# Another set of rank offsets for the scheduler of a Fourier filter with a gated convolution

## The chip, the cores and the metric

The kernel runs on one core of a Trainium2 chip. The metric is the device time of one execution, in microseconds (us). A profile is one further execution recorded by the hardware profiler; its span runs from the first to the last instruction.

## What is computed

x has 8 batches of 3200 positions and 256 channels. Each batch goes through a real Fourier transform along the positions, a complex 256x256 product with a bias, a soft threshold and the transform back; then through a gated product:

```python
X = np.fft.rfft(x, axis=1)
Yr = Xr @ w_r - Xi @ w_i + b_r
Yi = Xr @ w_i + Xi @ w_r + b_i
Y = soft(Yr, 0.01) + 1j * soft(Yi, 0.01)
y = np.fft.irfft(Y, n=3200, axis=1)
gate = sigmoid(sum over k < 5 of conv_w[k] * y shifted by 4 - k)
out = (gate * (y @ w_val)) @ w_out
```

`w_val`, `conv_w` and `w_out` arrive as float64 and are turned into float32 on the chip by integer steps.

## The kernel before, in words

The transform of 3200 points is split into 64 times 50. For each batch b there are three parts.

- **p1**, 8 pieces: x is loaded (`load`, L577), multiplied by `f1_sb` (L583), copied to SBUF by ScalarE (L588) and stored to `a_dram` (L597).
- **p2**, 13 units, u = 0 to 12, of two frequencies each (the last has one): `a` is loaded back once for two units (L615), multiplied by `f2_sb` (`s2`, L634), split into a high and a low half (L684 to L696), multiplied by the complex weights (`mix_sum` L709, `mix` L704; in the last unit L667 and L668), biased (L715, L718), thresholded (L722, L724), and for every second unit multiplied by `g1_sb` (`s1i`, L747; the last unit L739), copied (L758, L755) and stored to `z_dram` (L765).
- **p3**, 8 blocks k of four: z is loaded (L788), multiplied by `g2_sb` (`positions`, `s2i`, L803) and copied to `y_sb` (L810), of which there is one for all batches. `taps` forms the convolution for one or two blocks (first tap on ScalarE L857, four more for each half on VectorE L860, sigmoid L871). `gated` splits y into high and low (helper `split`, L360 and L362), forms val (`matrix`, L835, or whole in float32, L831), multiplies it by the gate on VectorE (L902), splits that product and multiplies it by `w_out` (project, L835 or L831), copies it (L926, the last block L920) and stores it (L928, L924).

The program order on every engine is not written out by hand. `Plan` collects pieces (engine, modelled duration, what they need, which tile they open) and lays them in an order by a greedy list simulation: for each engine it takes, of the pieces that could start within a slack (20 ns on the computing engines, 50 ns on SP) of the earliest, the one with the smallest rank `at`. The engine whose piece starts first goes next. The rank is the unit's place, b * 13 + u, plus an offset from the dictionary `O`. The simulation also holds the slots of each tile kind (`SLOTS`; two for `ps_2`, which p1, z, y_p, val and project tiles share), eight DMAs under way, a limit on DMA backlog for pieces with a rank above -27, the price of going between quadrant and full-array matmuls (`SWITCH`), and a model of how the matrix engine's instructions are fetched: in packets of 256, asked for 130 instructions into a packet, at 5200 ns each plus a share of the DMA backlog.

Offsets have the name of the step: `p1` and `p1_step` for the first products, `load_x`, `load_a`, `load_z` for loads on SP, `s2`, `mix_sum`, `s1i` within p2, `p3` for the start of the third part, and relative to it `y` (split), `conv` (taps), `val`, `gate` (gate product and its split) and `project`. A name with a number belongs to that batch and is added. `later` ranks the float64 conversion, `turn` the making of `g1_sb`. `together` favours staying in quadrant mode, `stay` widens the slack in that mode, `hold` holds back a lone quadrant piece when fewer than `crowd` are near. `late_val` and `late_out` are indices into the list `LATE` of the blocks of batches 6 and 7, from which on val and project take the whole float32 weights; at 7 and 15 that is the last block of batch 6 and all of batch 7 for val, and the last block of batch 7 for project.

```python
lone = e == "PE" and sum(c[1]["mode"] == "q" for c in near) < O["crowd"]
if e == "PE" and mode == "q":
    stay = max(SLACK[e], 100 * min(O["stay"], 4.0))
...
start, p = min(near, key=lambda c: (c[1]["at"] + (0.0 if e != "PE" or c[1]["mode"] != "q" else -O["together"] if mode == "q"
                                                   else O["hold"] if lone else 0.0), c[0]))
...
p1(b, u, (b - 1) * T + O["p1"] + O.get(f"p1_{b}", 0.0) + u * O["p1_step"])
...
start = (b + 1) * T + O["p3"] + O.get(f"p3_{b}", 0.0)
...
positions(b, k, start + (i - 1) * T / NB)
```

Of the kernel before, what the change touches and what calls it, by code (L numbers as in the profile page):

```python
# [83 lines left out]
class Plan:  # L84
# [11 lines left out]
    def add(self, at, engine, busy, fn, uses=(), sets=(), new=None, delay=None, mode="r", kb=0, chain=None, extra=0, moves=1, ways=16, ins=0):  # L96
        n = len(self.pieces)
        before = set()
        for key in uses:
            before |= set(self.writers.get(key, ()))  # L100
        for key in sets:
            before |= set(self.readers.get(key, ())) | set(self.writers.get(key, ()))
        for key in uses:
            self.readers.setdefault(key, []).append(n)
        for key in sets:
            self.writers[key], self.readers[key] = [n], []
        p = dict(n=n, at=round(at, 5), engine=engine, busy=busy, fn=fn, before=before, new=new or {}, mode=mode, kb=kb, extra=extra, moves=moves, ways=ways, ins=ins,
                 tiles={key[:2] for key in (*uses, *sets)}, delay=busy + LAND[engine] if delay is None else delay)
        p["behind"] = {self.last[chain]} if chain in self.last else set()
        if chain:  # L110
            self.last[chain] = n
        self.pieces.append(p)
        return n

    def order(self):
# [42 lines left out]
        while len(done) < len(pieces):  # L158
            best = None
            for e in engines:  # L160
# [13 lines left out]
# [4 lines that stand above are left out]
                    near = [c for c in could if c[0] <= first + (stay if c[1]["mode"] == "q" else SLACK[e])]  # L178
                start, p = min(near, key=lambda c: (c[1]["at"] + (0.0 if e != "PE" or c[1]["mode"] != "q" else -O["together"] if mode == "q"
                                                                   else O["hold"] if lone else 0.0), c[0]))  # L180
                if best is None or start < best[0]:
# [68 lines left out]
def act(n, kind="copy"):  # L250
# [3 lines left out]

NU = (NT + 1) // 2
T = float(NU)
O = {'stay': -42.085,
     'crowd': -50.453,
     'hold': 7.335,
     'together': 155.775,  # L260
     'later': 18.484,
     'load_x': 192.178,
     'p1': -1.787,
     'p1_step': 1.293,
     'load_a': -41.005,
     's2': -2.447,
     's1i': 2.145,
     'p3': 2.825,
     'load_z': -29.254,
     'y': 3.704,  # L270
     'conv': 5.188,
     'val': 5.514,
     'gate': -19.992,
     'project': 8.565,
     'late_val': 7.079,
     'late_out': 15.503,
     'turn': -153.706,
     'mix_sum': -0.971,
     'p1_1': -89.715,
     'load_x_1': 85.875,  # L280
     'p1_2': 25.498,
     'p3_6': -1.759,
     'p3_7': -0.606,
     'y_7': 18.885,
     'conv_7': -29.176,
     'val_7': 13.441,
     'gate_7': -17.01,
     'project_7': 13.598,
     'p3_1': -0.93,
     'p1_3': -6.723,  # L290
     'p3_0': 0.056}
WARM = 4, 1, 19
SLOTS = {"x": 3, "zl": 3, "y_hl": 2, "s1": 3, "a": 2, "xs": 2, "sx": 2, "xz": 1, "yb": 2, "tp": 3, "zst": 2,
         "acc": 2, "g_hl": 2, "o": 2, "ps_s2": 2, "ps_y": 1, "ps_k": 2, "ps_2": 2, "a_dram": 2, "z_dram": 2}
# [6 lines left out]
def fourier_filter_then_gated_conv(ctx: ExitStack, tc: tile.TileContext, x, w_r, w_i, b_r, b_i,  # L301
# [5 lines left out]
    dram = ctx.enter_context(tc.tile_pool(name="dram", bufs=2, space=bass.MemoryType.DRAM))  # L307
    LATE_VAL, LATE_OUT = set(LATE[int(O["late_val"]):]), set(LATE[int(O["late_out"]):])
    plan = Plan(SLOTS)
# [80 lines left out]
    def from_float64(at, n, views, uses, done, new=None, first=None):  # L390
# [34 lines left out]
        for k, (fn, busy) in enumerate(steps):  # L425
            def piece(k=k, fn=fn):
                if k == 0 and first:
                    first()
                fn()
            add(at + O["later"] + 0.12 * k, "DVE", busy, piece, uses, done, new if k == 0 else None, delay=busy + (130 if k == 12 else 0))  # L430

# [599 lines left out]
```

## Time and profile before

| | |
|---|---|
| three runs | 883.49, 883.22, 881.55 us (median 883.22) |
| profiled execution | 881.59 us, of which the span is 879.8 |
| mean granted clock of the matrix engine | 0.994 |
| busy: PE, DVE, ACT | 857.8, 759.1, 604.9 us |
| DMA | 163.34 MB, mean 186 GB/s |

PE is the matrix engine's matmuls, PEld its weight loads, which overlap them; DVE is VectorE, ACT ScalarE, POOL GpSimd, SP the engine whose queue issues most DMAs. L835 is line 835 of the kernel. A group of instructions is given as line, engine, operation, out<-in, shapes and count, then busy time and mean ns of one, then idle time of the engine before them and who ended it. A wait row reads: who waited, for whom, us in all, times, longest. A row of the timeline has start, length, engine, line and how often the operation follows itself. "issue" is time in which an engine waited for nothing that the profile shows. Ends of matmuls are modelled, so a busy PE may hide slack.

### The profile page before, as it was taken

The numbers are of one execution on the slowest core, as the hardware profiler recorded it, in microseconds if no ns is written. First come the engines' busy times: TensorE is split into PE (matmuls) and PEld (weight loads), VectorE is DVE, ScalarE is ACT, GpSimd is POOL, SyncE is SP. The second block draws the span as 40 slices with busy tenths as digits, with TensorE's granted clock in tenths as the row PEclk, the third lists the DMA queues.
The fourth block names the chain that finished last, engine by engine and source line by source line (L and its number), as shares of the span: only waits on it lengthen the run. The fifth ranks groups of instructions, "written<-read, shape, count | busy, mean of one in ns | idle before, by whom it ended". The sixth has DMA issues, their size and how long they took to land.

```text
span 879.8 us, 24544 instructions
## 1 busy us (share of the span) xinstructions
PE 857.8 (97%) x10400; PEld 745.5 (85%) x10400; DVE 759.1 (86%) x1143; ACT 604.9 (69%) x928; POOL 3.8 (0%) x11
## 2 busy tenths in 40 slices
PE   7999999999999999999999999999999999998997
PEld 3778788878999898898899889898899999998775
DVE  2346888999989996999879997899969999899796
ACT  2456666977677766877667776877658775875664
POOL 0000000000000000000000000000100000000000
PEclk9999999999999999999999999999999999999999
DMA  6878886786554476565855576646746353423522
GB/s 212 253 244 253 240 269 197 265 251 199 165 184 146 148 218 212 177 185 172 272 168 171 175 237 205 218 122 208 244 133 202 104 171 94 142 103 110 186 76 94
DMA packets 105289, 163.34 MB, mean 186 GB/s; under 512 B 9690, under 2 KB 78172, under 8 KB 105180
## 3 DMA queue, kind: packets, MB, share of 16 engines
q1 hardware_dynamic: 103764, 158.43, 58.1%
q10 hardware_dynamic: 1416, 3.34, 1.2%
q8 instruction: 82, 1.34, 0.6%
q14 instruction: 27, 0.22, 0.1%
HBM read 82.05 MB, written 79.69 MB: 184 GB/s over the span
## 4 chain that ended last, share of the span: by engine, by line
PE 78%; DVE 15%; DMA 3%; ACT 2%; issue 1%; SPq 0%; ACTq 0%; DVEq 0%
PE y_ps L704 14%; PE o_ps L835 12%; PE v_ps L835 11%; PE s L634 9%; PE z_ps L747 8%; PE k_bank L709 7%; PE y_p L803 6%; DVE acc L860 6%; PE p L583 5%; DMA x<-in_x 2%; PE warm L951 1%; DVE acc L902 1%; PE v_ps L831 1%; DMA f_sb<-in_f 1%; DVE gated L362 1%
## 5 line engine op out<-in xcount | busy, mean ns | idle before, releaser
L860 DVE SCALAR_TENSOR_TENSOR acc<-y_sb,cw_sb,acc 128x800 f32<-128x800 f32 (+1 forms) x264 | 258.7, 1017 | 11.4 <-ACT acc L857 11.2
L704 PE MATMUL y_ps<-w_sb,xs 128*128 128x256 f32 x1152 | 157.7, 286 | 0.7 <-DVE yb L718 0.7
L835 PE MATMUL o_ps<-gated,wo_sb 128*128 128x400 f32 x756 | 153.5, 352 | 0.0
L704 PEld LDWEIGHTS y_ps<-w_sb,xs 128*128 128x128 f32 x1152 | 144.3, 190 | 8.6 <-issue 3.9
L835 PEld LDWEIGHTS o_ps<-gated,wo_sb 128*128 128x128 f32 x756 | 135.6, 189 | 3.4 <-issue 1.0
L835 PE MATMUL v_ps<-y_hl,wv_sb 128*128 128x400 f32 x660 | 130.6, 346 | 1.1 <-ACT y_sb L810 1.1
L634 PEld LDWEIGHTS s<-f_sb,a 128*128 128x128 f32 x800 | 100.3, 191 | 24.9 <-issue 19.0
L835 PEld LDWEIGHTS v_ps<-y_hl,wv_sb 128*128 128x128 f32 x660 | 118.7, 188 | 2.1 <-ACT y_sb L810 1.3
L634 PE MATMUL s<-f_sb,a 128*128 128x128 f32 x800 | 111.9, 280 | 1.3 <-DVE xs L692 1.2
L747 PE MATMUL z_ps<-tp,g_sb 64*64 64x256 f32 x1536 | 93.7, 380 | 0.0
L688 ACT CAST xs<-s 128x512 fp32r<-128x512 f32 x96 | 56.2, 586 | 43.0 <-PE y_ps L704 28.1
L709 PE MATMUL k_bank<-w_sb,xs 128*128 128x256 f32 x576 | 85.3, 283 | 0.4 <-DVE yb L715 0.4
L722 ACT ACTIVATE tp<-yb,nlam 128x512 f32<-128x512 f32 (+1 forms) x104 | 73.6, 708 | 16.5 <-DVE yb L718 9.0
L718 DVE TENSOR_TENSOR yb<-y_ps,yb 128x512 f32<-128x512 f32 x96 | 65.4, 681 | 19.9 <-PE y_ps L704 19.7
L747 PEld LDWEIGHTS z_ps<-tp,g_sb 64*64 64x64 f32 x1536 | 57.1, 133 | 27.1 <-issue 5.8
L360 ACT CAST gated<-acc 128x800 fp32r<-128x800 f32 x63 | 54.2, 861 | 37.1 <-DVE acc L902 33.5
L709 PEld LDWEIGHTS k_bank<-w_sb,xs 128*128 128x128 f32 x576 | 74.8, 188 | 5.1 <-issue 1.1
L926 ACT COPY o<-o_ps 128x800 f32<-128x800 f32 x63 | 51.9, 823 | 38.0 <-PE o_ps L835 37.8
L803 PEld LDWEIGHTS y_p<-g_sb,zl 50*64 50x64 f32 x4096 | 66.1, 135 | 13.9 <-issue 5.1
L902 DVE TENSOR_TENSOR acc<-v_ps,acc 128x800 f32<-128x800 f32 x64 | 62.9, 983 | 16.9 <-PE v_ps L835 14.1
L724 DVE SCALAR_TENSOR_TENSOR tp<-yb,tp 128x512 f32<-128x512 f32 (+1 forms) x104 | 68.8, 661 | 7.7 <-ACT tp L722 7.4
L803 PE MATMUL y_p<-g_sb,zl 50*64 50x50 f32 x4096 | 71.8, 220 | 3.4 <-issue 2.2
(80 smaller groups left out, 1028.4 us busy)
## 6 DMA issues: line engine op xcount, KB each, us to landing
zl<-z_dram SPq DMA_DIRECT2D x128, 200.0 KB
out<-o SPq DMA_DIRECT2D x63, 400.0 KB
a_dram<-s SPq DMA_DIRECT2D x120, 208.0 KB
a<-a_dram SPq DMA_DIRECT2D x96, 256.0 KB
z_dram<-z_t SPq DMA_DIRECT2D x48, 512.0 KB
x<-in_x SPq DMA_DIRECT2D x120, 200.0 KB
a_dram<-s ACTq DMA_DIRECT2D x8, 208.0 KB
x<-in_x ACTq DMA_DIRECT2D x8, 200.0 KB
```

The lines of the kernel that those rows point to most:

```text
L634: nc.tensor.matmul(spec()[:, c, :, i, :], tl[ka][:, i0 + i, c * P:(c + 1) * P], f2_of(i), start=True, stop=True)
L688: nc.scalar.copy(out=tl[kx][:, 0:512], in_=tl[k2].rearrange("p a b -> p (a b)"))
L704: nc.tensor.matmul(p[:, 1 - r, :], xm(hx, c, r), w_sb[:, m, hw, c, :], start=k == 0, stop=k == 5)
L709: nc.tensor.matmul(p, sm(hx, c), w_sb[:, 0, hw, c, :], start=k == 0, stop=k == 5)
L718: add(at + 0.2, "DVE", dve(2 * D), lambda: nc.vector.tensor_tensor(out=yb(), in0=tl[ky], in1=yb(), op=ALU.add), [ky + (0,)], [kb + (0,)])
L722: nc.scalar.activation(out=buffer(kt, "tp", [P, 2, D])[:, 0:n], in_=tl[kb][:, 0:n], func=AF.Relu, bias=nlam)
L724: add(at + 0.2, "DVE", dve(n * D), lambda: nc.vector.scalar_tensor_tensor(out=tl[kt][:, 0:n], in0=tl[kb][:, 0:n], scalar=LAM, in1=tl[kt][: ...
L747: nc.tensor.matmul(p[e * HP:(e + 1) * HP, i, j * D:(j + 1) * D], g[i * HP:(i + 1) * HP, r, e * HP:(e + 1) * HP], tl[kts[j]][i * HP:(i + 1) ...
L803: nc.tensor.matmul(pv[h][e * HP:(e + 1) * HP, c, m, :], zt[half(h), m, c * P + e * HP:c * P + (e + 1) * HP], g2_sb[half(h), :], start=True ...
L835: nc.tensor.matmul(p[:, e, 0:TB], w[:, hw, c, e * P:(e + 1) * P], src(hy, c), start=n == 0, stop=n == 5)
L860: nc.vector.scalar_tensor_tensor(out=acc(c), in0=y_of(c, j), scalar=cw_sb[:, c, j:j + 1], in1=acc(c), op0=ALU.mult, op1=ALU.add)
L902: add(at + own("gate", b), "DVE", dve(2 * TB), lambda: nc.vector.tensor_tensor(out=gate(), in0=hn(tl[kv][:, :, 0:TB]), in1=gate(), op=ALU. ...
```

## The change

Only numbers in `O` change. The pieces, their instructions and sizes, the slots and the simulation stay as they are; the order in which the simulation lays them out is another. `late_val` and `late_out` keep their values, so the same blocks take the whole weights.

```diff
-O = {'stay': -42.085,
-     'crowd': -50.453,
-     'hold': 7.335,
-     'together': 155.775,
-     'later': 18.484,
-     'load_x': 192.178,
-     'p1': -1.787,
-     'p1_step': 1.293,
-     'load_a': -41.005,
-     's2': -2.447,
-     's1i': 2.145,
-     'p3': 2.825,
-     'load_z': -29.254,
-     'y': 3.704,
-     'conv': 5.188,
-     'val': 5.514,
-     'gate': -19.992,
-     'project': 8.565,
+O = {'stay': -60.503,
+     'crowd': -102.979,
+     'hold': 18.379,
+     'together': 205.778,
+     'later': 86.272,
+     'load_x': 124.016,
+     'p1': -1.441,
+     'p1_step': 1.544,
+     'load_a': -11.084,
+     's2': -1.909,
+     's1i': 2.258,
+     'p3': 0.441,
+     'load_z': -50.245,
+     'y': 8.904,
+     'conv': 9.838,
+     'val': 5.628,
+     'gate': -16.483,
+     'project': 7.913,
      'late_val': 7.079,
      'late_out': 15.503,
-     'turn': -153.706,
-     'mix_sum': -0.971,
-     'p1_1': -89.715,
-     'load_x_1': 85.875,
-     'p1_2': 25.498,
-     'p3_6': -1.759,
-     'p3_7': -0.606,
-     'y_7': 18.885,
-     'conv_7': -29.176,
-     'val_7': 13.441,
-     'gate_7': -17.01,
-     'project_7': 13.598,
-     'p3_1': -0.93,
-     'p1_3': -6.723,
-     'p3_0': 0.056}
+     'turn': -139.497,
+     'mix_sum': -0.639,
+     'p1_1': -49.829,
+     'load_x_1': 76.138,
+     'p1_2': 56.402,
+     'p3_6': 1.34,
+     'p3_7': 3.039,
+     'y_7': 106.034,
+     'conv_7': -43.292,
+     'val_7': 14.22,
+     'gate_7': -25.153,
+     'project_7': 14.981,
+     'p3_1': 0.545,
+     'p1_3': -48.761,
+     'p3_0': -0.433}
```

## The prediction

> **What bounds the kernel now.** I read the page first, then busy time by stretches, then who waited for whom on the matrix engine and on VectorE in the last 80 us, then the instructions around the waits found there. The page's head gives the span and the shares:
>
> ```profile
> span 879.8 us, 24544 instructions
> PE 857.8 (97%) x10400; PEld 745.5 (85%) x10400; DVE 759.1 (86%) x1143; ACT 604.9 (69%) x928; POOL 3.8 (0%) x11
> ```
>
> The stretches (length, then busy time of PE, weight loads, DVE, ACT, POOL; then clock, DMA share and GB/s) show three regimes:
>
> ```profile
> 0.00:80.00 80.00, 71.24 (x484) 49.63 (x484) 31.47 (x56) 34.50 (x64) 1.14 (x9) 0.96 0.81 238
> 80.00:120.00 40.00, 39.30 (x396) 31.59 (x393) 33.14 (x76) 26.82 (x47) 0.00 (x0) 1.00 0.83 259
> 120.00:160.00 40.00, 39.51 (x616) 33.50 (x615) 34.95 (x67) 27.38 (x48) 0.00 (x0) 1.00 0.74 221
> 160.00:240.00 80.00, 78.53 (x855) 67.59 (x850) 76.66 (x112) 59.88 (x91) 0.00 (x0) 1.00 0.71 218
> 240.00:720.00 480.00, 479.18 (x6195) 433.38 (x6195) 440.65 (x648) 355.43 (x542) 2.69 (x2) 1.00 0.60 184
> ...
> 720.00:760.00 40.00, 39.81 (x614) 37.20 (x616) 36.67 (x59) 25.24 (x40) 0.00 (x0) 1.00 0.44 139
> 760.00:800.00 40.00, 39.71 (x484) 36.72 (x480) 39.91 (x52) 30.63 (x43) 0.00 (x0) 1.00 0.29 100
> 800.00:824.00 24.00, 20.05 (x285) 17.50 (x278) 18.21 (x23) 12.81 (x17) 0.00 (x0) 0.93 0.48 159
> 824.00:872.00 48.00, 46.70 (x491) 36.12 (x489) 46.22 (x56) 30.87 (x41) 0.00 (x0) 1.00 0.30 106
> 872.00:880.00 8.00, 3.76 (x14) 2.22 (x13) 1.21 (x2) 1.32 (x2) 0.00 (x0) 0.93 0.27 102
> ```
>
> From 240 to 720 PE stands idle for 0.8 us of 480: PE bounds it. From 760 DVE is full (39.91 of 40), has a hole of 5.8 us between 800 and 824, and is nearly full again until 872 (46.22 of 48): the last batch's end is bound by DVE, with PE close beside it. The first 240 us hold 11.4 us of PE idle time, 8.8 of them in the first 80. A sequence can win only in those idle times and in what hides inside busy time. Who waited in the last 80 us, PE first, then DVE:
>
> ```profile
> PE z_ps L739 <- DVE acc L902: 2.9, 1, 2.9
> PE y_p L803 <- issue: 1.3, 2, 1.0
> ...
> DVE acc L860 <- ACT acc L857: 4.2, 2, 3.5
> DVE o L920 <- DMA out<-o: 3.7, 1, 3.7
> ```
>
> **What the change leaves alone.** The instructions are the same, so the sum of their durations is too. Of the 35 offsets many cannot act. `stay` is negative in both, so the slack stays at 20 ns; with `crowd` below zero `lone` is never true and `hold` is unread; `together` (156, now 206) exceeds the difference of priorities among work that is ready together. `y_7` is unread, since batch 7's val products all lie in the late list, which needs no split. The x loads are last on SP in both (124 and more against at most about 130 for the last output, which comes batches later), `turn` is first in both, `p1_1` stays ahead of, and `p1_2` behind, everything ready beside it. `later` pushes the float64 conversion behind still more work, but at 25.6 it already stood behind nearly all of batch 1's middle (13 to 26), and DVE idles 6.9 us between 80 and 120. Each of these I cost at nothing.
>
> **What it does change, as places in one batch of 13 units.** Adding `p3` to the offset, in units from the batch's start: positions 2.8 to 0.4, val 8.3 to 6.1, project 11.4 to 8.4 (all earlier on PE); the y split 6.5 to 9.3 and the taps 8.0 to 10.3 (later on ACT and DVE); the gate product -17.2 to -16.0. For batch 6 with its own offset: y 4.8 to 10.7, taps 6.3 to 11.6, val 6.6 to 7.4, positions 1.1 to 1.8, project hardly. Batch 7: positions 2.2 to 3.5, taps -21.8 to -30.0, val and project two later, still in the same order. First products (p1) are spread over 7 steps of 1.54 and not 1.29. On SP the z loads go from behind the next batch's a loads to ahead of them, and batch 0's a loads come under the backlog limit.
>
> A unit in time: the single last-z product closes the p2 part of batches 5 and 6 at these starts, 99.4 us apart, so 7.6 us a unit.
>
> ```profile
> 610.67 0.59 PE L739 MATMUL z_ps<-tp,g_sb 128*128 128x256 f32 x2
> 710.07 0.59 PE L739 MATMUL z_ps<-tp,g_sb 128*128 128x256 f32 x2
> ```
>
> **SP.** PE never waits for a landing behind the start: its waits for DMA are x at 1.7 and f at 1.2 us in all, both before 60 us, and batch 0's a loads, with a priority of -11 and up, still go ahead of the f2 parts beside them (0.1 and up). The cover for the later a loads is the queue of ready val and project work. If it is gone, one late load costs what the f transfer cost, 1.2. I take 0, with 0 to +1.2.
>
> ```profile
> PE p L549 <- DMA x<-in_x: 1.7, 2, 1.0
> ...
> PE k_bank L469 <- DMA f_sb<-in_f: 1.2, 1, 1.2
> ```
>
> **Mode runs in the middle.** PE alternates between full-array pieces and quadrant pieces (p1, z, y_p). What one excursion costs is read from neighbouring starts:
>
> ```profile
> 691.50 1.05 PE L634 MATMUL s<-f_sb,a 128*128 128x128 f32 x8
> 692.31 2.42 PE L835 MATMUL v_ps<-y_hl,wv_sb 128*128 128x400 f32 x12
> ...
> 696.68 1.05 PE L634 MATMUL s<-f_sb,a 128*128 128x128 f32 x8
> 697.66 1.15 PE L803 MATMUL y_p<-g_sb,zl 50*64 50x50 f32 x64
> ...
> 720.34 1.96 PE L747 MATMUL z_ps<-tp,g_sb 64*64 64x256 f32 x32
> 722.22 0.97 PE L709 MATMUL k_bank<-w_sb,xs 128*128 128x256 f32 x6
> ```
>
> ```profile
> 300.58 1.96 PE L747 MATMUL z_ps<-tp,g_sb 64*64 64x256 f32 x32
> 302.36 1.04 PE L583 MATMUL p<-x,f_sb 50*64 50x512 f32 x8
> ```
>
> The s piece lasts 0.81 us until a full-array piece starts and 0.98 until a quadrant piece does; z lasts 1.78 until p and 1.88 until a full-array piece. An excursion so costs 0.17 + 0.10 = 0.27 us. Between the two L739 rows above there are nine runs, from this first one (618.57) to the y_p at 697.66:
>
> ```profile
> 618.57 1.09 PE L583 MATMUL p<-x,f_sb 50*64 50x512 f32 x8
> ```
>
> That is 2.4 us a batch. Nine runs serve 22 quadrant pieces, and the two slots of `ps_2`, which every one of these pieces and every val and project tile needs, keep a run to two or three pieces. The new steps bring p1 and positions nearly in line: p1 at -1.4, 0.1, 1.6, 3.2 ..., positions at -1.2, 0.4, 2.1, 3.7 ..., so that pairs get likelier. I take one run fewer in each of four settled batches, -4 x 0.27 = -1.1 us; bounds one run more or two fewer in seven batches, +1.9 to -3.8.
>
> **Issue stalls.** Long trains of small matmuls run the queue dry: after 157 records of y_p this row waits 1.02 us for nothing but issue.
>
> ```profile
> 817.57 2.77 PE L803 MATMUL y_p<-g_sb,zl 50*64 50x50 f32 x157
> 821.35 0.78 PE L803 MATMUL y_p<-g_sb,zl 50*64 50x50 f32 x35 [1.02 <-issue]
> ```
>
> Over the span PE lost 2.2 us so:
>
> ```profile
> PE y_p L803 <- issue: 2.2, 5, 1.0
> ```
>
> An order rated over three packet times should break up the worst train; I take -0.4 (a third of the tail's 1.3), bounds -2.2 to +2.2, since as many new ones can arise. The Trainium skill's page "Runtime: NRT & Kernel Launch", section "Instruction fetch mechanics", has it that crossing a block of instructions is mostly hidden. By that rule this term would be 0 and the sum 0.4 us higher; the 1.02 us row speaks against it for dense trains.
>
> **The tail.** Batch 7's positions need all of z, and batch 6's taps must have read `y_sb`, which exists once. The wait of DVE is this one:
>
> ```profile
> 823.90 4.90 DVE L860 SCALAR_TENSOR_TENSOR acc<-y_sb,cw_sb,acc 128x800 f32<-128x800 f32 x5 [3.55 <-ACT acc L857]
> ```
>
> With batch 6's taps and splits 5.3 to 5.9 units (40 us and more) later in rank, batch 7's p2 instructions go ahead of them on DVE, the last z comes earlier, and some of batch 6's DVE work is left to fill the hole while z goes to memory and back. I take half the 3.55, -1.8 us; bounds: both waits gone, -3.55 - 2.9 = -6.5, and two further waits of the kind of L739's, +5.9. What is late next is the val tile's slot, and DVE itself, which has 1.8 us left between 824 and 872.
>
> Startup and fill (0 to 240): p1 of batch 3 goes from 17.5 to -24 and starts runs of its own. I take 0, between -2.6 (all the idle time from 80 to 240) and +1.4 (five more runs).
>
> **The sum**: -1.1 - 0.4 - 1.8 = -3.3 us. The profiled execution took 881.59 (span 879.8 and 1.8 around it) and would take 878.3; the median of the three runs is 883.22, 1.6 higher, so the forecast is 879.9.
>
> **Rivals.** *Slower: val tiles park in the two slots.* Val waits for its y split, the taps come after, and a val tile holds one `ps_2` slot until L902 has multiplied it, which needs taps and sigmoid. Before, taps (8.0) were ahead of val (8.3); after, val can run when the split is done (9.3) and the taps stand at 10.3: 0.9 units, 7 us, in which one of two slots may be held and PE waits for each evacuation. The trace has one such case, the 2.9 us of L739. It decides when DVE is full while the tile waits, as in 760 to 800. Two more in the tail, or one in each of two full batches, give 883.2 + 5.9 = 889; one gives 886. Against it: 240 to 720 has almost no such wait, and every other val finds its taps within what DVE can spare (39 of 480 us idle). Chance 0.28.
>
> *No change.* The hole is a round trip (last z, store, load, y_p, copy, first tap) that no rank shortens, and the middle is full: 883.2. That much of the list is unread, and the changed sequence is then nearly the old one, is the same case. Chance 0.22.
>
> *Much faster.* PE's busy 97% may hide slack: from 240 to 720 weights load for 433 of 480 us. If a better order reclaimed a tenth of the 46 us between, and the tail both waits, it is -4.6 - 6.5, 872; with half the tail, 875. The Trainium skill's page "Perfetto Trace Analysis", section "Identifying the Most-Contended Engine", judges PE by weight-load share, 85% here, and not by matmul share; that rule points this way. Against it, from the page's groups (busy, mean ns):
>
> ```profile
> L747 PE MATMUL z_ps<-tp,g_sb 64*64 64x256 f32 x1536 | 93.7, 380 | 0.0
> ...
> L747 PEld LDWEIGHTS z_ps<-tp,g_sb 64*64 64x64 f32 x1536 | 57.1, 133 | 27.1 <-issue 5.8
> ```
>
> z alone streams 36.6 us longer than its weights load, over the span, and any order keeps that. Chance 0.10.
>
> **How the numbers follow.** Forecast 0.40, much faster 0.10, no change 0.22, slower 0.28. A measurement of this kernel tells about 0.2%, 1.8 us. Faster 0.50, same 0.22, slower 0.28. The likeliest case alone is 877 to 881.5; for eight in ten the range runs from 874 (into the much faster case) to 888 (two slot waits short of their full price), which holds also the bounds of the runs term.
>
> **What would show it.** Right: between 800 and the end the wait of L860 for L857 at about half, the last L739 starting some us before 804, eight runs between two L739 rows, the y_p issue wait under 2. Wrong: PE idle time above 2 us between 240 and 720, or new waits for L902 (slots); the last L739 at 804 or later; a DVE idle time before 760 larger than now, with more taps behind it.

## The result, and the profile after

The changed kernel is slower: 885.48 us (median of 12, 880.81 to 892.98) beside 880.45 for the kernel before, a ratio of 1.0056 [1.003, 1.0082]. Its profiled execution took 887.27, of which the span is 885.3, at a mean granted clock of 0.986 where the kernel before had 0.994. The time lies in the forecast range of 874 to 888, and the direction is the opposite of the forecast. The head of the page after:

```profile
span 885.3 us, 24513 instructions
PE 860.8 (97%) x10400; PEld 747.2 (84%) x10400; DVE 759.8 (86%) x1143; ACT 602.8 (68%) x928; POOL 4.4 (1%) x11
```

The shares say nothing of the 5.5 us: PE is at 97% in both. The stretches do (length, then busy time of PE, weight loads, DVE, ACT, POOL; then clock, DMA share, GB/s). After:

```profile
120.00:160.00 40.00, 37.57 (x588) 29.88 (x591) 31.57 (x61) 26.15 (x44) 0.00 (x0) 1.00 0.65 200
160.00:200.00 40.00, 38.51 (x461) 31.29 (x454) 38.19 (x56) 31.09 (x47) 0.00 (x0) 0.96 0.76 236
...
240.00:720.00 480.00, 475.70 (x6192) 430.04 (x6191) 440.75 (x646) 353.64 (x536) 3.30 (x2) 1.00 0.60 183
...
760.00:800.00 40.00, 39.79 (x511) 37.10 (x511) 39.68 (x59) 28.78 (x45) 0.00 (x0) 1.00 0.29 98
800.00:840.00 40.00, 37.27 (x455) 32.04 (x455) 33.53 (x39) 25.58 (x32) 0.00 (x0) 0.91 0.46 151
840.00:880.00 40.00, 38.79 (x341) 30.16 (x340) 36.24 (x45) 22.75 (x31) 0.00 (x0) 1.00 0.20 73
```

Between 120 and 160 PE was idle for 0.5 us before and for 2.4 now. In the settled stretch, 240 to 720, it was idle for 0.8 us before and for 4.3 now, and one wait makes more than half of that. The waits of the matrix engine, over the whole span (who, for whom, us in all, times, longest):

```profile
PE v_ps L835 <- ACT tp L722: 2.6, 1, 2.6
PE y_p L803 <- issue: 1.9, 5, 0.6
...
PE p L583 <- ACT y_sb L810: 1.6, 1, 1.6
PE y_p L803 <- DVE acc L902: 1.5, 1, 1.5
PE k_bank L709 <- ACT xs L695: 1.5, 1, 1.5
```

The 2.6, the 1.6 for L810's copy and the 1.5 for L695 are not in this list of the kernel before. VectorE's waits have a line that was not there at all, a step of the float64 conversion (L401) waiting for the matrix engine; the longest wait of L860 for L857, which is the tail's, is still whole (3.55 before):

```profile
DVE acc L860 <- ACT acc L857: 11.3, 8, 3.7
...
DVE st L401 <- PE y_p L803: 3.2, 1, 3.2
```

Idle time alone misses what shows as stretched matmuls, because their ends are modelled. I therefore took from each window the matrix work that started in it at its price back to back (a piece of s 0.81 us, 12 mixes 1.40, z 1.73, y_p 0.97, 12 matmuls of val or project 2.17, a piece of p1 0.91) and call the rest *lost*. By windows, in us, each from one profile:

| lost in | 40–60 | 60–120 | 120–200 | 640–680 | 800 to the end |
|---|---|---|---|---|---|
| before | 6.6 | 4.8 | 7.8 | 2.8 | 16.5 |
| after | 2.9 | 6.2 | 12.0 | 6.2 | 16.8 |
| difference | -3.7 | +1.4 | +4.2 | +3.4 | +0.3 |

The differences sum to +5.6; the spans differ by 5.5. Outside these windows the largest differences are +1.0 (0 to 40) and -0.9 (200 to 240). So two places are to be explained, the fill (120 to 200) and one near 660, against a gain between 40 and 60. A second profile of the same order (new_unread, below) loses 11.7 in 120 to 200, much the same, but 5.5 in 40 to 60 and 3.9 in 640 to 680, so these two differences are not firm.

**The fill.** Here is the wait of L401 step by step (start, length, engine, line, operation; idle time before it in brackets). VectorE, after:

```profile
130.64 0.68 DVE L718 TENSOR_TENSOR yb<-y_ps,yb 128x512 f32<-128x512 f32 x1
134.48 0.43 DVE L401 TENSOR_SCALAR st<-st 128x512 int32<-128x512 int32 x1 [3.15 <-PE y_p L803]
...
136.15 0.42 DVE L691 TENSOR_TENSOR sx<-s,sx 128x256 f32<-128x256 f32 x1
```

ScalarE, after:

```profile
132.24 0.59 ACT L688 CAST xs<-s 128x512 fp32r<-128x512 f32 x1
136.60 0.40 ACT L695 CAST xs<-sx 128x256 fp32r<-128x256 f32 x1 [3.77 <-DVE sx L691]
136.91 0.82 ACT L810 COPY y_sb<-y_p 128x800 f32<-128x800 f32 x1
```

The matrix engine, after:

```profile
133.26 1.15 PE L803 MATMUL y_p<-g_sb,zl 50*64 50x50 f32 x64
134.23 1.92 PE L747 MATMUL z_ps<-tp,g_sb 64*64 64x256 f32 x32
137.78 1.09 PE L583 MATMUL p<-x,f_sb 50*64 50x512 f32 x8 [1.64 <-ACT y_sb L810]
```

Batch 0's positions now begin at 133.26. Before, the conversion's last step on VectorE and the first y_p of the matrix engine stood here:

```profile
143.66 0.69 DVE L362 TENSOR_TENSOR wo_sb<-st,wo_sb 128x512 fp32r<-128x512 f32 x1
...
149.80 1.10 PE L803 MATMUL y_p<-g_sb,zl 50*64 50x50 f32 x64
```

The conversion of `w_out` ran from 125 to 144 before and from 128 to 147 after. Both use the three `zl` slots: the conversion for its loaded tile and two work tiles, the positions for their z. Before, the conversion was over when the first y_p came. Now its second work tile takes the slot of a z tile and must wait until y_p has read it, at 134.2. In DVE's program the sum L691 of p2 stands behind that step, ACT's L695 behind L691, the copy of y_p (L810) behind L695, and the copy alone gives back a `ps_2` slot that PE's next first product needs. By rank the conversion stands behind all the work around it, and it held that work up.

The simulation does not see this wait. Its function `opens` compares each tile that a piece opens with the slots as they were before the piece, and the first step of the conversion opens both work tiles, so both are counted on the same slot. In the layout of the changed order four tiles lie in the three `zl` slots from 122.6 to 128.5 us of the plan; in the layout of the order before there are never more than three around its conversion.

**Near 660.** The matrix engine, after:

```profile
657.28 1.68 PE L704 MATMUL y_ps<-w_sb,xs 128*128 128x256 f32 x12
661.56 3.49 PE L835 MATMUL v_ps<-y_hl,wv_sb 128*128 128x400 f32 x12 [2.59 <-ACT tp L722]
664.85 1.53 PE L634 MATMUL s<-f_sb,a 128*128 128x128 f32 x8
666.13 0.95 PE L709 MATMUL k_bank<-w_sb,xs 128*128 128x256 f32 x6
```

Its weight loads at the same moment, and two stretches around it:

```profile
661.56 2.95 PEld L835 LDWEIGHTS v_ps<-y_hl,wv_sb 128*128 128x128 f32 x11 [2.68 <-issue]
```

```profile
655.00:660.00 5.00, 3.96 (x104) 3.82 (x97) 4.96 (x6) 4.91 (x7) 0.00 (x0) 1.00 0.83 246
660.00:665.00 5.00, 3.44 (x13) 3.41 (x13) 3.54 (x5) 1.59 (x2) 0.00 (x0) 0.74 0.70 258
```

The matmul row names a semaphore of ACT, the weight-load row says issue: nothing was waited for. The records of the instruction queue (82 transfers of 16 KB, 256 instructions each) settle it. PE's stops that end just behind such a landing lie whole multiples of 256 matmuls, weight loads and semaphore records apart. PE stopped exactly at the first instruction of a packet, whose transfer began at 659.09 and landed at 660.12; PE went on 1.4 us later. The transfer began 5.7 us after PE had passed the request point, by which I mean the instruction 319 places ahead of the packet's first one, where the simulation has the packet asked for; the median over all packets is 2.7 (2.5 in the kernel before). The granted clock is 0.74 from 660 to 665, and the 12 matmuls took 3.29 us to the next start instead of 2.17. Summed over the packets at whose edge PE had run dry, it is 4.6 us before (longest 1.24) and 8.5 after (longest 2.87), counted from the start of the last instruction to the start of the packet's first one, so each holds an ordinary step of some 0.2 us; PE's idle time alone is 2.4 before and 5.3 after. Sums of packet waits below are counted from start to start unless they are called idle time; single waits are idle time. The Trainium skill, page "Runtime: NRT & Kernel Launch", section "Instruction fetch mechanics", says that crossing into the next 16 KiB block of 256 instructions is mostly hidden. These rows agree on the size of a block; one block here cost 2.6 us, and the slow clock followed it.

### The profile page after: what moved, and what is told of

The parts are those of the page before. It is cut to its first block, busy times and chain, and to the rows that moved or that the text cites. A ratio compares the mean times of both kernels' runs of the same rounds, so it can differ in the third digit from the quotient of the medians.

```text
span 885.3 us, 24513 instructions
## 1 busy us (share of the span) xinstructions
PE 860.8 (97%) x10400; PEld 747.2 (84%) x10400; DVE 759.8 (86%) x1143; ACT 602.8 (68%) x928; POOL 4.4 (1%) x11
## 4 chain that ended last, share of the span: by engine, by line
PE 83%; DVE 11%; DMA 2%; ACT 2%; issue 1%; ACTq 0%; SPq 0%; DVEq 0%
PE y_ps L704 14%; PE o_ps L835 13%; PE v_ps L835 12%; PE s L634 10%; PE z_ps L747 8%; PE k_bank L709 7%; PE y_p L803 7%; PE p L583 5%; DVE acc L860 5%; PE v_ps L831 2%; PE warm L951 1%; DVE acc L902 1%; DMA x<-in_x 1%; DVE gated L362 1%; PE p L549 1%
## 5 line engine op out<-in xcount | busy, mean ns | idle before, releaser
L860 DVE SCALAR_TENSOR_TENSOR acc<-y_sb,cw_sb,acc 128x800 f32<-128x800 f32 (+1 forms) x264 | 261.4, 1018 | 11.5 <-ACT acc L857 11.3
L704 PE MATMUL y_ps<-w_sb,xs 128*128 128x256 f32 x1152 | 153.6, 282 | 0.3 <-issue 0.2
L709 PE MATMUL k_bank<-w_sb,xs 128*128 128x256 f32 x576 | 91.4, 294 | 2.1 <-ACT xs L695 1.5
L803 PEld LDWEIGHTS y_p<-g_sb,zl 50*64 50x64 f32 x4096 | 67.7, 136 | 13.9 <-issue 3.7
L803 PE MATMUL y_p<-g_sb,zl 50*64 50x50 f32 x4096 | 74.2, 222 | 4.8 <-issue 1.9
L715 DVE TENSOR_TENSOR yb<-k_bank,bias_sb 128x512 f32<-128x512 f32 x96 | 65.4, 681 | 12.9 <-PE k_bank L709 8.0
L718 DVE TENSOR_TENSOR yb<-y_ps,yb 128x512 f32<-128x512 f32 x96 | 65.6, 683 | 8.6 <-PE y_ps L704 7.9
L360 ACT CAST y_hl<-y_sb 128x800 fp32r<-128x800 f32 x55 | 47.3, 860 | 32.2 <-PE v_ps L835 31.9
L871 ACT ACTIVATE acc<-acc 128x800 f32<-128x800 f32 (+1 forms) x66 | 55.5, 852 | 18.3 <-DVE acc L860 18.1
```

Source lines behind the costliest of these rows:

```text
L360: nc.scalar.copy(out=high(), in_=src())
L704: nc.tensor.matmul(p[:, 1 - r, :], xm(hx, c, r), w_sb[:, m, hw, c, :], start=k == 0, stop=k == 5)
L709: nc.tensor.matmul(p, sm(hx, c), w_sb[:, 0, hw, c, :], start=k == 0, stop=k == 5)
L715: nc.vector.tensor_tensor(out=buffer(kb, "yb", [P, 2, D]), in0=tl[kk].rearrange("p (a d) -> p a d", a=1).to_broadcast([P, 2, D]), in1=bias ...
L718: add(at + 0.2, "DVE", dve(2 * D), lambda: nc.vector.tensor_tensor(out=yb(), in0=tl[ky], in1=yb(), op=ALU.add), [ky + (0,)], [kb + (0,)])
L803: nc.tensor.matmul(pv[h][e * HP:(e + 1) * HP, c, m, :], zt[half(h), m, c * P + e * HP:c * P + (e + 1) * HP], g2_sb[half(h), :], start=True ...
```

## The experiments

**Which offsets act.** Laying out the order with one offset at a time changed shows that in both kernels stay, crowd, hold, together, later, load_x, load_a, load_z, gate, turn, p1_1, load_x_1, p1_2, y_7 and gate_7 leave the order of PE, DVE, ACT and SP as it is (set back all fifteen together, they do change the order of the changed kernel). It is s2, mix_sum, s1i, p1, p1_step, p3, y, conv, val, project and most of the numbered ones that act. s2 changes the order already at the 47th piece of PE. From 790 us of the plan on, both sets lay the rest in the same order, and from 760 on the plan ends at the same time with either.

**1. new_unread.** Ten offsets of the changed kernel set back, so that its order is the same.

```diff
-O = {'stay': -60.503, 'crowd': -102.979, 'hold': 18.379, 'together': 205.778, 'later': 86.272, 'load_x': 124.016,
+O = {'stay': -42.085, 'crowd': -50.453, 'hold': 7.335, 'together': 155.775, 'later': 18.484, 'load_x': 192.178,
...
-     'gate': -16.483,
+     'gate': -19.992,
...
-     'turn': -139.497,
+     'turn': -153.706,
...
-     'y_7': 106.034,
+     'y_7': 18.885,
...
-     'gate_7': -25.153,
+     'gate_7': -17.01,
```

> The changed kernel with ten offsets set back (stay, crowd, hold, together, later, load_x, gate, turn, y_7, gate_7); every engine's order is the changed kernel's. All theories: the changed kernel's time, about 5 us over the kernel before. It shows which losses recur in a second profile. Theory fill (the loss lies between 60 and 200 us, where the changed kernel loses some 6 us more than the kernel before): again 8 to 10 us lost between 120 and 200. Theory packets (the loss is a late packet of matrix-engine instructions, as in the 2.6 us wait at 658 to 661): again a wait of 2 us or more near 658.

Measured: 884.04 us, 1.0028 [1.0009, 1.0048]; the profile loses 11.7 us in 120 to 200 and 3.9 in 640 to 680. These ten do nothing, the slowdown is there without them, and what it measures varies by some 0.3% from one set of runs to another. Both causes recur in this second profile: L401 waits 3.2 us for y_p, and the same packet near 660 stops PE for 2.3 us, this time at the full clock:

```profile
660.81 2.35 PE L835 MATMUL v_ps<-y_hl,wv_sb 128*128 128x400 f32 x12 [2.29 <-ACT tp L722]
```

```profile
660.00:665.00 5.00, 4.19 (x29) 4.19 (x29) 3.44 (x6) 3.37 (x6) 0.00 (x0) 1.00 0.70 257
```

So of the 6.2 us lost near 660 in the first profile, some 2.3 came with the slow clock and not with the packet alone.

**2 and 3. old_180_new and new_180_old.** Each piece carries both ranks; the layout goes by one set until PE, DVE and ACT have all passed 180 us of the plan, then by the other.

```diff
-        p = dict(n=n, at=round(at, 5), engine=engine, ...
+        p = dict(n=n, at=np.broadcast_to(np.round(at, 5), 2), engine=engine, ...
...
-            best = None
+            best = None; side = (FIRST_SET + sum(min(free[e] for e in ("PE", "DVE", "ACT")) >= c for c in CUTS)) % 2
```

> Old ranks until 180 us of the plan, new ranks from there. The scheduler's own simulation ends 3 us before that of the kernel before. Theory fill: that gain comes through, 877 to 879 us. Theory packets: the settled stretch has the new ranks, a late packet of 2 us or more turns up between 240 and 720, and the time is 881 to 884.

> New ranks until 180 us of the plan, old ranks from there. The scheduler's own simulation ends 1 us before that of the kernel before. Theory fill: 882 to 885 us, 3 to 5 over the kernel before, with 8 us or more lost between 120 and 200. Theory packets: 879 to 881, no wait of 2 us between 240 and 720.

Measured: old until 180, then new, 880.7 us, 0.9993 [0.9968, 1.0018]; new until 180, then old, 884.67 us, 1.0029 [1.0009, 1.0049]. The slowdown sits in the first 180 us of the order. Lost in 120 to 200: 7.9 with the old beginning, 13.9 with the new one. A gain behind 180 was too small for these runs to tell; with the new ranks behind 180 the late packet is there too (2.1 us of idle time at 656.7), as theory packets had it for that run, and it may have eaten the gain.

**4, 8, 11 and 16. new_shift120, new_shift60, old_shift60 and old_shift120.** The order is unchanged; the first 30 (or 15) warming matmuls at the start are made as two halves each, which moves every later instruction of PE 120 (or 60) places along its packets.

```diff
-        for _ in range(n):
-            nc.tensor.matmul(pw...[:, 0:2 * P], tl[ki][:, 0:P], tl[ki][:, 0:2 * P], start=True, stop=True)
+        for lo, hi in halves(n, 30):
+            nc.tensor.matmul(pw...[:, lo:hi], tl[ki][:, 0:P], tl[ki][:, lo:hi], start=True, stop=True)
```

> The changed kernel with its order, and 120 more instructions on the matrix engine at the start (each of the 30 warming matmuls as two halves), so that every later packet of 256 instructions begins 120 instructions earlier in the work. Theory fill: the changed kernel's time within 1 us, 884 to 887. Theory packets: the wait near 658 is gone and, unless another takes its place, the time is 3 to 5 us lower, 880 to 882.

> The changed kernel with 60 more instructions at the start. Theory packets: where the packets begin decides, so the time lies anywhere between the 880 of the shift by 120 and the 885 of the changed kernel, and the wait at 660 is changed by over 1 us. Theory fill: 884 to 885.5, and 12 us lost between 120 and 200 in both theories.

> The kernel before with 60 more instructions on the matrix engine at the start. Theory packets: the place of the packets matters in any order; 3 to 12 us slower, with packet waits that sum to 8 us or more against 4.6. Rival: only the new order has trains dense enough; 880 to 883.

> The kernel before with 120 more short matrix instructions at its start and its order unchanged. Theory (the new order's settled part and start are really cheaper, and where the packets begin adds or takes a few us in every kernel): ratio 0.997 to 1.003, so that at this same start the own-tile kernel (0.9934) stays ahead by 0.5 to 0.9%. Rival (the own-tile kernel's lead is mostly the luck of its packets at this start, which the old order would have as well): ratio 0.995 or below.

Measured, changed kernel: at 120 880.14 us, 0.9988 [0.9965, 1.0011]; at 60 895.42 us, 1.0145 [1.0103, 1.0188]. Kernel before: at 60 884.66 us, 1.0038 [1.0013, 1.0062]; at 120 880.25 us, 0.9995 [0.998, 1.001]. The same order, moved along its packets, spans 1.6% in the changed kernel and 0.4% in the one before. The 895 lies outside what either theory had for it. At 60 the waits of the changed kernel for nothing but issue are these:

```profile
PE y_p L803 <- issue: 6.1, 5, 2.9
PE y_ps L704 <- issue: 4.0, 1, 4.0
...
PE z_ps L747 <- issue: 2.1, 1, 2.1
```

At 120 the packet waits of the changed kernel sum to 4.1 us instead of 8.5, and 640 to 680 loses 2.2 instead of 6.2; 120 to 200 still loses 14.0. One packet wait of 2.8 us remains, now at 558. So the two causes are apart: a shift moves the packet waits, and the wait of L401 for y_p (3.2 us) is there at every shift of the changed order. The fill's loss as a whole is not free of the shift, because a packet can be late there as well: at 60 the changed order loses 17.8 in it, 2.1 of them for a packet at 162, and the order before loses 9.6 and 11.0 at 60 and 120, with a packet wait of 2.0 and 2.1 near 160, where it lost 7.8. In the order before, packets cost 5.4 us of idle time at 60 and 3.2 at 120, against 2.4.

**5 and 9. new_own_tile and old_own_tile.** The order stays; the second work tile of `w_out`'s conversion is taken from the slots of the output tiles ("o"), which are not yet in use, and no longer from `zl`.

```diff
-                     lambda: [buffer(key, "zl", [P, MB * D]) for key in keys[1:]])
+                     lambda: [buffer(keys[1], "zl", [P, MB * D]),
+                              buffer(keys[2], *(("o", [P, 2 * TB]) if name == "w_out" else ("zl", [P, MB * D])))])
```

> The changed kernel, order and instructions the same; only the second work tile of the conversion of w_out lies in a slot of the tag o (free until the first project) and not in one of the three zl slots. Theory fill: the 3.15 us for which VectorE stood at 131 to 134 before a conversion step until y_p had read its zl tile are gone, with them ScalarE's 3.8 us and the matrix engine's 1.6; 120 to 200 loses 9 to 10 us and not 12, the time is 2 to 3 us under the changed kernel's, 881 to 882.5. Theory packets alone: no change, 884 to 885.5.

> The kernel before with the same edit of one tile (second work tile of w_out's conversion in a slot of the tag o), order the same. Theory: the edit cures a wait that only the new order has, because there the first positions take their zl slot before the conversion does; so the kernel before stays as it is, 880 to 883. Rival: one tile fewer in the zl slots helps any order; then it is 3 to 8 us faster, 874 to 878, as with the new order.

Measured: on the changed kernel 877.1 us, 0.9953 [0.9932, 0.9974], faster than the kernel before; on the kernel before 880.6 us, 0.999 [0.9974, 1.0007], nothing. VectorE at the same place, new_own_tile:

```profile
129.96 0.68 DVE L718 TENSOR_TENSOR yb<-y_ps,yb 128x512 f32<-128x512 f32 x1
130.56 0.42 DVE L401 TENSOR_SCALAR st<-st 128x512 int32<-128x512 int32 x1
...
132.22 0.42 DVE L691 TENSOR_TENSOR sx<-s,sx 128x256 f32<-128x256 f32 x1
```

L691 starts 2.3 us after L718, where it was 5.5; the copy of y_p follows, ScalarE in new_own_tile:

```profile
132.67 0.41 ACT L695 CAST xs<-sx 128x256 fp32r<-128x256 f32 x1 [0.52 <-DVE sx L691]
133.79 0.83 ACT L810 COPY y_sb<-y_p 128x800 f32<-128x800 f32 x1 [0.71 <-PE y_p L803]
```

The matrix engine's work in 120 to 200, changed kernel, then with the tile of its own:

```profile
120.00:200.00 80.00, 76.07 (x1045) 61.17 (x1045) 69.76 (x116) 57.23 (x90) 0.00 (x0) 0.98 0.71 218
```

```profile
120.00:200.00 80.00, 78.50 (x1133) 65.26 (x1133) 74.45 (x123) 60.11 (x94) 0.00 (x0) 1.00 0.77 240
```

Lost in 120 to 200 falls from 12.0 to 6.7. The edit takes away one wait in one place and touches no rank, and it only helps the order in which y_p comes before the conversion's end: the shared slot is shown as the cause of the fill's loss. Of the 5.3 us, 1.6 are PE's wait for L810's copy and some 1.6, by estimate, the granted clock, 0.98 over 80 us and now 1.00. The median falls by more than that window's 5.3 us: its packets waited 5.7 us in all instead of 8.5 and 640 to 680 lost 3.0 instead of 6.2, probably because with other waits PE meets its packets at other moments; that part is not the slot's alone, for the same packet was late again in own_tile_table.

**6. old_180_new_shift120.** Edits 2 and 4 together.

> Old ranks until 180 us of the plan, new ranks after, and 120 more instructions at the start. If the two losses are separate and add up, this has neither: 876 to 878, 3 to 5 under the kernel before, with no packet wait of 2 us near 657. If shifting only moves the wait about (as it did to 558 with the new ranks alone), 880 to 881.5.

Measured: 881.61 us, 0.9999 [0.9977, 1.0022]. Its packet waits sum to 8.5 us (PE stood idle for 2.5 at 159 and 2.5 at 557), so what one shift gave to one order it did not give to another. No gain behind 180 is seen here either.

**7. new_no_out.** 63 of the 64 output stores of the changed kernel are left out, so that less data travels beside the instruction packets.

```diff
-        add(kind, "SP", 400, lambda: nc.sync.dma_start(out=dst, in_=tl[ko]), [ko + (0,)], (), kb=400)
+        add(kind, "SP", 400, lambda: None, [ko + (0,)], (), kb=400)
```

> The changed kernel without its output stores but for the last block's, so 63 stores of 400 KB fewer; the matrix engine's instructions stay. Theory packets, in the form that a packet comes late because its transfer queues behind data: the waits for packets sum to half or less of 8.5 us and the one near 660 is under 1 us; time 3 to 5 us lower. If a packet takes a fixed time that the dense train outruns, the wait near 660 stays at 2 to 3 us.

Measured: 885.21 us, 1.0033 [1.0007, 1.0058]. The wait of the fill remains, and near 660 PE still stood idle for 1.6 us for a packet whose transfer began 4.3 us after the request point, with the median at 2.6. PE's idle time for packets is 5.0 in all, against 5.3. So the output stores are not the whole of what made that transfer late. What else does is open.

**10, 14 and 15. own_tile_table, own_tile_table_shift120 and old_table.** The first sigmoid of ACT loads a table, 1.28 us, in the fill; the changed kernel shows it with the work behind it (ScalarE, after):

```profile
169.68 1.28 ACT L871 ACT_TABLE_LOAD   x1
...
171.75 0.39 ACT L695 CAST xs<-sx 128x256 fp32r<-128x256 f32 x1
```

PE's 1.5 us for L695 in the list of waits above is this. One sigmoid of 128x1 is put on ACT after its fifth load of x, when ACT has nothing to do.

```diff
-            engines[h][1].dma_start(out=xt[half(h), :], ...)
+            (engines[h][1].dma_start(out=xt[half(h), :], ...), (u, h) == (4, 1) and nc.scalar.activation(out=early, in_=nlam, func=AF.Sigmoid))
```

> The changed kernel with the own tile, and one sigmoid of a 128x1 tile on ScalarE after its first five loads, so that the only table load is the first one. Theory: the 1.28 us table load at the first sigmoid holds up ScalarE's cast and, behind it, the matrix engine for 1.5 us near 170; both go, 1 to 3 us under the own tile alone, 874 to 876. Rival: something else holds the matrix engine there; 876.5 to 878.

> Own tile, early sigmoid and 120 more instructions. With the own tile alone the early sigmoid brought no gain; its profile had the 1.5 us wait at 170 gone and a packet wait of 2.7 us at 656. If that packet wait ate the gain, then with the packets begun elsewhere the early sigmoid shows: 1 to 2 us under own tile with shift 120, 873 to 876. If the early sigmoid itself is worth nothing: 876.5 to 878.5.

> The kernel before with the early sigmoid. In it the table load at 164 stands ahead of the 1.1 us for which v_ps waited for ScalarE at 169. If the early sigmoid is worth what the matrix engine waited: 879 to 880.5 where the kernel before has 881. If a gain there is given back later: 880.5 to 882.

Measured: 879.62 us, 0.998 [0.9962, 0.9998]; with the shift of 120 877.44 us, 0.9948 [0.9925, 0.9971]; on the kernel before 883.69 us, 1.0011 [0.9988, 1.0035]. PE's 1.5 us for L695 are gone from the list (in the kernel before the 1.1 us for L810's copy), and none of the three is faster than the same kernel without the edit (0.9953, 0.9934, 1). In own_tile_table another wait is back:

```profile
PE v_ps L835 <- ACT tp L722: 2.4, 1, 2.4
```

That is the packet near 656. It can account for the first of the three, and not for the other two. In 120 to 200 each of the three profiles loses 0.7 us less than its partner (6.8 to 6.1, 6.7 to 6.0, 7.8 to 7.1), half of the wait that went, and 0.7 us is less than these runs can tell. So the gain of 1 to 3 us that I expected did not come; why the wait gave only half is open.

**12 and 13. own_tile_shift120 and own_tile_shift60.** Edits 5 and 4 together.

> The changed kernel with the own tile and 120 more instructions at the start. If the 4 us by which the shift helped the changed kernel come from packets and add to the tile's gain: 872 to 875. If they came from the same place in the fill: 876 to 878.

> The changed kernel with the own tile and 60 more instructions at the start. If the shift by 60 costs through late packets on its own (it cost 10 us on the changed kernel): 884 to 889, with packet waits that sum to 10 us or more. If that cost came from the fill, where the conversion's wait and the packet wait met: 877 to 880.

Measured: 877.45 us, 0.9934 [0.9909, 0.9959], the best of all; and 886.06 us, 1.0046 [1.0021, 1.007]. All orders and shifts in one table (ratio to the kernel before):

| | as it is | shift 60 | shift 120 |
|---|---|---|---|
| order before | 1 | 1.0038 [1.0013, 1.0062] | 0.9995 [0.998, 1.001] |
| changed order | 1.0056 [1.003, 1.0082] | 1.0145 [1.0103, 1.0188] | 0.9988 [0.9965, 1.0011] |
| changed order, tile of its own | 0.9953 [0.9932, 0.9974] | 1.0046 [1.0021, 1.007] | 0.9934 [0.9909, 0.9959] |

Down a column, the tile is worth 1.0, 1.0 and 0.5% (9, 9 and 5 us). Along a row, the packets' place is worth 0.4 to 1.6%. With its own tile the changed order is 0.5 and 0.6% ahead of the order before in two columns and level with it in the third.

## Why the prediction was wrong, point by point

**The step that failed** is "Startup and fill (0 to 240)": "I take 0, between -2.6 (all the idle time from 80 to 240) and +1.4". Measured by lost time the fill cost +4.2 us in 120 to 200 and +1.4 in 60 to 120, and 40 to 60 gave 3.7 back; over all of 0 to 240 it is +2.0 (+2.8 in new_unread's profile), above the range, and with the tile of its own -3.6, below it. I had worked out that the positions move 2.4 units earlier on PE, and costed only p1's runs. What I did not ask is what the earlier z tiles collide with: `zl` is shared with the conversion, and the last step of the conversion and the first y_p lay 5 us apart in the trace of before (144.35 and 149.80), where the move is 16. The upper bound of +1.4 was made of mode switches alone, though a wait on a slot was the kind of cost that I had named elsewhere.

**The slower rival** had the right sign and the wrong place. Val tiles parked in `ps_2` are seen once, as PE's 1.5 us for L902 in the list of waits, where the kernel before had 2.9. Its chance of 0.28 for slower was too small, because it was the only mechanism behind it.

**Issue stalls**: I took -0.4, bounds ±2.2. The waits called issue did fall, from 2.2 to 1.9, as the sign named for it said, and the sign was the wrong one to watch: the longest packet wait was booked under a semaphore. Worked from the packets it is +3.9 (4.6 to 8.5; as idle time +3.0, from 2.4 to 5.3), outside the bounds. By the rule of the Trainium skill's page "Runtime: NRT & Kernel Launch", section "Instruction fetch mechanics", this term would have been 0; the shifts, worth up to 1%, speak against that.

**Mode runs**: the sign was right, and the count was too small. The last z (L739) closes a batch's p2 part; between the batches' rows the runs of quadrant pieces number 13, 10, 10, 9, 9, 9, 9 before and 13, 9, 8, 8, 8, 8, 7 after, eight less in 69 (forecast: one less in each settled batch). From batch 1's to batch 4's last z it is 301.4 us before, 300.1 after and 300.3 with the tile of its own: -1.3 and -1.1, with four runs fewer in these three batches; at 0.27 a run the four are the -1.1 that I had for four batches.

**The tail**: I took -1.8, and the wait of L860 for L857 at about half. The last z of batch 7:

```profile
L739 PE MATMUL z_ps<-tp,g_sb x16: 377/378/382, 117.8 to 806.4; 128*128 128x256 f32 x16
```

It is no earlier than before, and the two waits for L857 in the last 80 us are 4.4 in all, much as before (4.2). DVE's hole stays: 33.53 of 40 busy from 800 to 840. The reason lies in the layout: from 760 us of the plan on it ends at the same time with either set, so behind that point the later ranks of batch 6's taps and splits bring nothing. With the tile of its own the last z starts at 796.2, 8.0 us before the old one, and the end comes 4.8 earlier; lost behind 800 is 15.4, 1.1 less than before. The tail's gain is at most that. Of the signs named as wrong, PE idle above 2 us between 240 and 720 (4.3) and the last L739 at 804 or later (806.2) both came.

**What I costed at nothing**: stay, crowd, hold, together, later, y_7, load_x, turn, p1_1 and p1_2, each taken alone, do nothing (new_unread holds most of them). So do load_a and load_z, which I gave up to +1.2: PE's one wait for a landing behind the start is 0.4. That s2, mix_sum and s1i act I did not consider, and s2 alone reorders the start.

**The sum.** Forecast -3.3, measured +5.5 in the span. By lost time the gap of 8.8 splits so: startup and fill 2.0 (forecast 0), the packets' place near 660 3.8 (+3.4 where the issue term had -0.4), the tail 2.1 (+0.3 where I had -1.8), and the rest, which holds the mode runs, 0.8 (-0.3 where I had -1.1). The order without its collision gave -4.8 us of span and -0.47% [-0.68, -0.26], near the forecast, but in part by luck: -3.6 of the -4.8 lie in 0 to 240, where I had 0. The plan itself shows the gap: the simulation ends at 864.2 before and 859.9 after, 4.3 earlier; the chip is 10 us further behind the plan after than before. New lag arises in 60 to 200 (+6.2) and 640 to 700 (+3.8).

## What to carry to other kernels

When work moves earlier, look at every slot kind that it opens, and find in the trace who used that slot last: 5 us between two users is no cover when the move is 16 us. Check too that the scheduler's model counts every tile that a piece opens. In a kernel ordered to a fraction of a per cent, time the same order at some shifts of the instruction stream before a difference of 0.5% is ascribed to the order. A wait that names a long-finished engine is to be read again in the weight-load row.

## What the runs showed of the hardware

- A packet of 256 instructions began its transfer 2.5 to 3.0 us (median of each profile) after PE had passed the request point. In each of the 18 stops of over 1.5 us for a packet, in all profiles, it began 4.3 to 7.8 us after; where PE had run dry it went on 1.2 to 1.7 us after the packet landed. One wait cost up to 4.0 us (new_shift60). What delays a transfer is open.
- Sixty more instructions at the start, with the order kept, cost 0.9% (changed order, and with the tile of its own) and 0.4% (order before).
- A stop of PE of 2.6 us was followed by a granted clock of 0.74 from 660 to 665; the stop at the same packet in new_unread, 2.3 us, was followed by 1.00. A stop of 1.5 us for L695 was followed by 0.73 from 175 to 180 in the changed kernel, and by 1.00 in the one with the tile of its own, which has the same stop: the stop's length alone does not decide.
